# First norm block turned on VectorE, and first products of a pair accumulated in PSUM, in a linear-attention and Mish MLP block

## The chip, the cores and the metric

One NeuronCore of a Trainium2 chip runs one launch of the kernel. The metric is the device time of a run in microseconds. The kernel before took 486.94 us (median of 3 runs, 486.89 to 487.25).

## The reference

x is 2048 x 512 in float32; 32 heads of 16; the MLP has 1792 hidden units.

```python
mod = (_silu(c) @ w_mod).reshape(c.shape[0], 6, 1, -1)
sa, ca, ga, sb, cb, gb = (mod[:, 0], mod[:, 1], mod[:, 2], mod[:, 3], mod[:, 4], mod[:, 5])
h = _layernorm(x, axis=-1) * (1 + ca) + sa
x = x + ga * _A_ref(h, A_wqkv, A_wo)          # linear attention
h = _layernorm(x, axis=-1) * (1 + cb) + sb
x = x + gb * _B_ref(h, B_w1, B_b1, B_w2)      # Dense -> Mish -> Dense
```

In the attention, phi(t) is t + 1 for positive t and exp(t) otherwise, plus 1e-6; the numerator is phi(q) times the 16 x 16 sums of phi(k) v, the denominator phi(q) times the sums of phi(k).

## The kernel before

The rows are worked in four blocks b of 512 (0 to 3), each of four tiles t of 128 rows. Every matrix product is made of three products of halves: a float32 operand is split into an upper half "h" (a copy that ScalarE rounds, line 82) and a lower half "l" (the difference, on VectorE, line 88), and h·h, h·l and l·h are summed in a PSUM bank.

The order of the work is that of the program text: each engine takes its instructions in the order in which the code issues them. Side work is written as generators; `spawn` queues one and each `tick` (line 57) lets every queued generator issue its next step, so side work falls between units of TensorE. DMAs are issued by SyncE (SP), by GpSimd (POOL) and a few by ScalarE.

The stages, by the trace's clock: first layer norm, k, and the sums of phi(k) with x to 107 us; the q product of blocks 0 and 1 in seven products instead of eight (`q_sevens`, line 380) to 127; attention and output units `o_unit(b, t)` (line 920), with the q products of blocks 2 and 3 between them, to 205; the MLP of blocks 0 and 1 to 348, and of blocks 2 and 3 to the end.

An output unit multiplies the normalised q of a block, in halves qs (line 902), with a combined matrix m: twelve products of 128 x 512. The normalised q needs the reciprocal of the denominator, which goes out to DRAM as `rden_d` and comes back spread over partitions in four loads `rd` (`attend`, line 877; for blocks 2 and 3 SyncE issues them).

The second layer norm of block 0 is made by `norm_first` (line 927): ScalarE sums, VectorE and GpSimd make the scale, ScalarE applies it to `n_0_t`. Then the columns of the four tiles have to become rows for the MLP's products. For blocks 0 and 1, `transpose_f` (line 986) does that with four 128 x 128 turns on TensorE into a bank, from which ScalarE scales to `hf` (line 991). The table `order` (line 1080) says ahead of which output unit n = 4b + t each (block, quarter of the columns) is turned. For blocks 2 and 3, VectorE turns 32 x 32 squares into a tile `wide` (`turn`, line 235), four DMAs write them to DRAM (`spread`, line 241), four loads bring them back as rows (`load_squares`, line 249), and ScalarE scales (`turned_f`, line 982, line 256). The scaled quarters are split as b11, b21, b12, b22, and `columns` (line 996) makes the differences t1 to t4.

The hidden units are worked in pairs g of two tiles, the two blocks together by a scheme of seven products. In `pair_begin` (line 1151) the product a11·b11 goes into a bank `pa`; ScalarE copies it to SBUF as `u1`, the product a12·b21 goes into another bank, and VectorE adds the two (line 1158) before Mish. Later products s2·t2, s3·t3 and a22·t4 are accumulated onto `pa`, with ScalarE copies `u2` and `u3` between. `pair_unit` (line 1197) puts two units of the second matrix (`d_unit`, line 1116, or in the second half of the MLP `e_unit`, line 1347) between these products. `q_sevens` has the same scheme with `u1` in SBUF.

PSUM's eight banks have tags: acc four, h three, tp one.

Of the kernel before, what the change touches and what calls it, by code (L numbers as in the profile page):

```python
# [10 lines left out]
AF = mybir.ActivationFunctionType  # L11
# [14 lines left out]
def block_kernel(ctx: ExitStack, tc: tile.TileContext, x, wqkv, wo, w1, b1t, w2, c, wmodt, out):  # L26
# [352 lines left out]

    def q_sevens(side):  # L380

        pa, pc, u1, u2, u3 = {}, {}, {}, {}, {}

        def result(b, g, p, u):
            if u is not None:
                c = sb(f"cq_{b}_{g}")
                dve.tensor_tensor(c, p, u, op=ALU.add)
                p = c
            pq[b, g] = sb(f"q_{b}_{g}")
            spawn(phi(p, f"q_{b}_{g}", pq[b, g], u is not None))  # L390

        def copy(p, name):
            u = sb(name)
            act.activation(u, p, AF.Copy)
# [12 lines left out]
        for o in range(2):  # L407
            q_product(o, "s3", "t3", onto=pa[o])
            u3[o] = copy(pa[o], f"qu3_{o}")
        side(3)  # L410
        for o in range(2):
            result(0, 2 + o, q_product(o, "a22", "t4", onto=pa[o]), None)
        side(4)
        for o in range(2):
            pc[o] = q_product(o, "s1", "t1", ("h", "acc")[o])
            result(1, 2 + o, pc[o], u3[o])
        side(5)
        for o in range(2):
            q_product(o, "s4", "b22", onto=pc[o])
            result(1, o, pc[o], u2[o])  # L420
        side(6)
# [504 lines left out]

    def norm_first(t):

        yield
        sums = act_sums("n", 0, t, xt["r", 0, t])  # L930
        yield
        sums_eps("n", 0, t, sums)
        yield
        sums_shift("n", 0, t, sums)
        yield
        v = xt["n", 0, t] = sb(f"n_0_{t}")
        ln_apply("n", 0, t, xt["r", 0, t], v, act)

    def norm_each(b, t):

# [136 lines left out]
                tick()  # L1077
    act.preload_act_table_set("mish")

    order = {8: [(0, 0), (0, 2)], 9: [(0, 1)], 10: [(0, 3), (1, 0)], 11: [(1, 2)], 12: [(1, 1)], 13: [(1, 3)]}  # L1080
    for b in range(1, NB):
        for t in range(4):
            n = 4 * b + t
            for i, j in order.get(n, ()):
                transpose_f(i, j, "h")
                spawn(split_b(i, j, f"b{j // 2 + 1}{i + 1}"))
            if n in (12, 13):
                spawn(columns(0, n - 12, ("b11", "b12", "b21", "b22")))
            if n == 14:
                break  # L1090
            o_unit(b, t)
            if b == 1:
                spawn(norm_each(1, t))
            if n == 4:
                load_w2(0)
                load_w2(1)
            if n == 5:
                spawn(attend(3, 3, sp))
            if n == 7:
                spawn(w2_job(0))  # L1100
                spawn(w2_job(1))
                load_w2(2)
                load_w2(3)
            tick()
# [45 lines left out]

    def pair_begin(c0, g, tags):

        u1, pa = sb(f"u1_{g}"), product(g, "a11", "b11", tags[0])
        act.activation(u1, pa, AF.Copy)  # L1154
        c11, p = sb(f"c11_{g}"), product(g, "a12", "b21", tags[1])

        def result():
            add(c11, p, u1)
            yield
            yield from mish(c11, c0, 2 * g)  # L1160

        spawn(result())
        return pa

    def result_b(p, u, f):

# [4 lines left out]

    def pair_early(g, pa, tag):
# [34 lines left out]
    def two_pairs(c0, g0, g1, begun, between):  # L1209

        s0 = pair_early(g0, begun[0], "h")
        tick()
        pc = product(g1, "s1", "t1", "h")
        pair_middle(g0, *s0)
        tick()
        pa = begun[1]
# [322 lines left out]
```

## Time and profile before

| | us |
|---|---|
| median of the runs | 486.94 |
| the profiled execution | 487.57 |
| its span, first to last instruction | 485.9 |
| TensorE (PE) busy | 478.1 |
| VectorE (DVE) busy | 403.9 |
| ScalarE (ACT) busy | 305.6 |
| GpSimd (POOL) busy | 120.2 |

A row of a timeline has the start in us, the length in us, engine, line, operation, output<-inputs, shapes and count; in brackets, how long the engine had been idle and what ended that. PE is TensorE, DVE VectorE, ACT ScalarE, SPq the queue of SyncE that issues DMAs. Consecutive matmuls overlap, so the step from one start to the next counts. A row of the table of stages has, after the stage, its length, and the busy time of PE, of its weight loads (PEld), of DVE, ACT and POOL with counts, then the granted clock, the DMA engines' share and GB/s. A row of a DMA queue has packets, MB and the share of the 16 DMA engines.

### The profile page before, as it was taken

What the parts mean: (1) busy time and instruction counts of PE and PEld (TensorE: products, weight loads), DVE (VectorE), ACT (ScalarE), POOL (GpSimd) and SP (SyncE); (2) the same over time, 40 slices, a digit from 0 to 9 for tenths busy, and PEclk for the clock granted to TensorE, in tenths of its full rate; (3) what the DMA queues carried; (4) which work ended last, traced back from release to release, by engine and by line L of the source; (5) the groups of instructions that cost most, each with busy time, mean ns of one, the idle gap of its engine ahead of it and who ended that gap; (6) DMA issues with size and microseconds to landing.
All of it is one profiled execution on the core that took longest, in us unless ns stands there. A gap on an engine that the chain in (4) does not pass through costs nothing.

```text
span 485.9 us, 7068 instructions
## 1 busy us (share of the span) xinstructions
PE 478.1 (98%) x2322; PEld 390.8 (80%) x2322; DVE 403.9 (83%) x801; ACT 305.6 (63%) x551; POOL 120.2 (25%) x200
## 2 busy tenths in 40 slices
PE   7999999999999999999999999999999999999997
PEld 6688877767887888888888888888888888888887
DVE  6999898998999899988998883699345878879992
ACT  6786468755764979557887664795064667657600
POOL 3673121000022213113434225133011101454400
PEclk9999999999999999999999999999999999999999
DMA  8904859553865328258649539998352602687974
GB/s 305 379 10 82 200 102 263 203 146 92 272 172 152 92 74 258 86 175 282 219 148 266 168 108 263 378 327 209 126 149 78 125 16 65 152 194 156 235 153 108
DMA packets 81023, 84.90 MB, mean 175 GB/s; under 512 B 22705, under 2 KB 54969, under 8 KB 80986
## 3 DMA queue, kind: packets, MB, share of 16 engines
q1 hardware_dynamic: 55944, 49.17, 35.0%
q0 software_dynamic: 22784, 34.49, 26.6%
q10 hardware_dynamic: 2258, 0.79, 0.8%
q8 instruction: 18, 0.29, 0.2%
q14 instruction: 19, 0.16, 0.1%
HBM read 57.42 MB, written 24.91 MB: 169 GB/s over the span
## 4 chain that ended last, share of the span: by engine, by line
PE 83%; DMA 6%; DVE 6%; SPq 2%; ACT 1%; POOL 1%; issue 0%; DVEq 0%; ACTq 0%
PE p_a L1144 20%; PE p_s L1144 8%; PE oacc L75 5%; PE oacc L74 5%; PE oacc L76 5%; PE m L76 5%; PE m L74 5%; PE m L75 5%; PE o L74 3%; PE o L76 3%; PE o L75 3%; DMA sq_x<-wide_x 3%; DMA wm<-in_wmodt_dram 2%; PE pq_a L376 2%; PE pq L74 2%; PE pq L76 1%
## 5 line engine op out<-in xcount | busy, mean ns | idle before, releaser
L1154 ACT ACTIVATE u<-p_a 128x512 f32<-128x512 f32 x14 | 8.4, 599 | 29.5 <-PE p_a L1144 29.5
L776 POOL DMA_DIRECT2D wb<-w2d x14 | 9.8, 704 | 67.4 <-PE p_a L1144 16.9
L1149 DVE TENSOR_TENSOR cb<-p_s,u 128x512 f32<-128x512 f32 x28 | 19.2, 688 | 7.5 <-ACT u L1185 7.5
L1136 ACT ACTIVATE ub<-cb,b1c 128x512 f32<-128x512 f32 x28 | 20.1, 720 | 6.8 <-DVE cb L1149 6.7
L199 POOL TENSOR_TENSOR rs_n<-rs_n,half 128x1 f32<-128x1 f32 x16 | 9.8, 611 | 55.7 <-DVE rs_n L225 42.8
L1179 ACT ACTIVATE u<-p_a 128x512 f32<-128x512 f32 x12 | 7.2, 599 | 25.0 <-PE p_a L1144 25.0
L1435 POOL DMA_DIRECT2D wt_m<-w2t x20 | 14.0, 702 | 25.4 <-PE m L76 17.0
L889 POOL DMA_DIRECT2D rden_d<-rden x2 | 1.5, 736 | 60.1 <-DVE rden L887 60.1
L782 POOL DMA_DIRECT2D w2b<-w2d x20 | 10.6, 538 | 20.6 <-PE oacc L76 14.5
L1111 ACT ACTIVATE u<-p_a,b1c 128x512 f32<-128x512 f32 x14 | 9.6, 688 | 8.7 <-PE p_a L1144 8.6
L1149 DVE TENSOR_TENSOR c<-p_a,u 128x512 f32<-128x512 f32 x14 | 9.5, 688 | 5.7 <-PE p_a L1144 5.0
L1185 ACT ACTIVATE u<-p_a 128x512 f32<-128x512 f32 x14 | 8.3, 591 | 6.9 <-PE p_a L1144 6.5
L290 DVE SCALAR_TENSOR_TENSOR ku<-e_k,relu_k 128x512 f32<-128x512 f32 x16 | 11.3, 708 | 1.5 <-ACT relu_k L288 1.5
L290 DVE SCALAR_TENSOR_TENSOR q<-e_q,relu_q 128x512 f32<-128x512 f32 x16 | 10.7, 690 | 1.2 <-ACT relu_q L288 1.2
L199 POOL TENSOR_TENSOR rs_x<-rs_x,half 128x1 f32<-128x1 f32 (+1 forms) x10 | 7.8, 786 | 15.1 <-DVE rs_x L194 14.3
L190 DVE BATCH_NORM_STATS2 st_x<-x 128x6 f32<-128x512 f32 x13 | 8.8, 677 | 3.1 <-DMA x<-in_x_dram 3.1
L913 DVE TENSOR_TENSOR r<-o,r 128x512 f32<-128x512 f32 x16 | 10.9, 680 | 0.5 <-PE o L76 0.5
L287 ACT ACTIVATE e_k<-pk 128x512 f32<-128x512 f32 x16 | 9.4, 586 | 2.7 <-PE pk L76 2.7
L901 DVE SCALAR_TENSOR_TENSOR q<-q,rd 128x512 f32<-128x512 f32 x16 | 10.5, 691 | 0.2 <-DMA rd<-rden_d 0.2
L1127 DVE TENSOR_TENSOR r<-oacc,r 128x256 f32<-128x256 f32 x8 | 3.4, 425 | 8.8 <-PE oacc L76 8.8
L175 DVE SCALAR_TENSOR_TENSOR wm<-wm,sc_row 128x512 f32<-128x512 f32 x16 | 10.5, 688 | 0.0
L299 POOL DMA_DIRECT2D ku<-ku x8 | 7.2, 940 | 13.5 <-DVE ku L290 13.5
(1580 smaller groups left out, 1898.7 us busy)
## 6 DMA issues: line engine op xcount, KB each, us to landing
wm<-in_wmodt_dram SPq DMA_DIRECT2D x24, 256.0 KB, 5.8
w1p<-in_w_dram SPq DMA_DIRECT2D x24, 256.0 KB, 4.3
w2b<-w2d POOLq DMA_DIRECT2D x20, 256.0 KB, 6.8
wt_m<-w2t POOLq DMA_DIRECT2D x20, 256.0 KB, 3.6
r<-in_x_dram SPq DMA_DIRECT2D x16, 256.0 KB, 2.9
x<-in_x_dram SPq DMA_DIRECT2D x15, 256.0 KB, 4.7
w2r<-in_w_dram SPq DMA_DIRECT2D x14, 256.0 KB, 7.7
wb<-w2d POOLq DMA_DIRECT2D x14, 256.0 KB, 3.5
```

The costliest lines, as they stand in the source:

```text
L74: pe.matmul(o, st[0], mv[0], start=start, stop=False)
L75: pe.matmul(o, st[0], mv[1], start=False, stop=False)
L76: pe.matmul(o, st[1], mv[0], start=False, stop=stop)
L175: dve.scalar_tensor_tensor(t, t, 1.0, row, op0=ALU.mult, op1=ALU.mult, accum_out=mc[:, i:i + 1])
L199: pool.tensor_tensor(y, y, half[:, lo:hi], op=ALU.pow)
L290: dve.scalar_tensor_tensor(dst, e, 1.0, r, op0=ALU.min, op1=ALU.add)
L782: pool.dma_start(w2s[f][i], w2d[f // 2, i][:, f % 2, :])
L913: dve.tensor_tensor(r, p, r, op=ALU.add)
L1136: act.activation(u, p, AF.Mish, bias=b1c[:, f:f + 1])
L1144: pe.matmul(p, st, mv, start=onto is None and c == 0 and i == 0, stop=c == 1 and i == 2, skip_group_check=onto is not None)
L1149: dve.tensor_tensor(out, p, u, op=ALU.add)
L1435: pool.dma_start(v, w2t[g][:, :, SUM[name], :])
```

## The change

Three things are changed.

First, block 0's second norm is turned on VectorE, spread and loaded back, as blocks 2 and 3 are; `norm_first` starts one tick earlier and issues the turns, the spread and the loads of squares; the table `order` is rewritten, and block 1 is still turned on TensorE. Second, ScalarE's copy of a11·b11 goes into the PSUM bank of the second product, a12·b21 is accumulated onto it, and the sum on VectorE goes; so in `q_sevens` and in every pair. In a pair, a12·b21 moves behind the first unit of the second matrix (in the first two pairs behind the output units that stand there), and s1·t1 behind s2·t2. Third, the split b12 of block 1's first half, which no product uses, is left out; the differences t1 to t4 of blocks 0 and 1 are issued after the output unit of their place rather than ahead of it.

```diff
     def q_sevens(side):
...
         for o in range(2):
             pa[o] = q_product(o, "a11", "b11", "h")
-            u1[o] = copy(pa[o], f"qu1_{o}")
+            p11[o] = ps(("h", "tp")[o], f"pq_11_{o}")
+            act.activation(p11[o], pa[o], AF.Copy)
         side(0)
         for o in range(2):
-            p = q_product(o, "a12", "b21", ("h", "tp")[o])
-            result(0, o, p, u1[o])
+            q_product(o, "a12", "b21", onto=p11[o])
+            result(0, o, p11[o], None)
             q_product(o, "s2", "t2", onto=pa[o])
...
     def norm_first(t):
-        yield
         sums = act_sums("n", 0, t, xt["r", 0, t])
         yield
         sums_eps("n", 0, t, sums)
         yield
         sums_shift("n", 0, t, sums)
-        yield
-        v = xt["n", 0, t] = sb(f"n_0_{t}")
+        v = sb(f"n_0_{t}")
         ln_apply("n", 0, t, xt["r", 0, t], v, act)
+        yield
+        turn("n", 0, t, v)
+        if t == 3:
+            yield
+            spread("n", 0)
+            for _ in range(3):
+                yield
+            for j in (0, 2, 1, 3):
+                load_squares("n", 0, j)
...
-    order = {8: [(0, 0), (0, 2)], 9: [(0, 1)], 10: [(0, 3), (1, 0)], 11: [(1, 2)], 12: [(1, 1)], 13: [(1, 3)]}
+    order = {9: [(0, 0), (0, 2)], 10: [(1, 0)], 11: [(0, 1), (1, 2)], 12: [(0, 3), (1, 1)], 13: [(1, 3)]}
...
             for i, j in order.get(n, ()):
-                transpose_f(i, j, "h")
-                spawn(split_b(i, j, f"b{j // 2 + 1}{i + 1}"))
-            if n in (12, 13):
-                spawn(columns(0, n - 12, ("b11", "b12", "b21", "b22")))
+                if i:
+                    transpose_f(i, j, "h")
+                else:
+                    turned_f(i, j)
+                if (i, j // 2) != (1, 0):
+                    spawn(split_b(i, j, f"b{j // 2 + 1}{i + 1}"))
             if n == 14:
                 break
             o_unit(b, t)
+            if n in (12, 13):
+                spawn(columns(0, n - 12, ("b11", "b12", "b21", "b22")))
...
     def pair_begin(c0, g, tags):
-        u1, pa = sb(f"u1_{g}"), product(g, "a11", "b11", tags[0])
-        act.activation(u1, pa, AF.Copy)
-        c11, p = sb(f"c11_{g}"), product(g, "a12", "b21", tags[1])
...
+        pa, p11 = product(g, "a11", "b11", tags[0]), ps(tags[1], f"p11_{g}")
+        act.activation(p11, pa, AF.Copy)
+        return pa, p11
...
+    def pair_first(c0, g, p11):
+        m = mish(product(g, "a12", "b21", onto=p11), c0, 2 * g)
+        next(m)
+        spawn(m)
+
+    def pair_early(c0, g, begun, tag):
+
+        pa, p11 = begun
         u2 = sb(f"u2_{g}")
-        pc = product(g, "s1", "t1", tag)
+        pair_first(c0, g, p11)
         product(g, "s2", "t2", onto=pa)
         act.activation(u2, pa, AF.Copy)
+        pc = product(g, "s1", "t1", tag)
         return pa, pc, u2
...
     def pair_unit(c0, g, odd, between):
         begun = pair_begin(c0, g, ("tp" if odd else "h", "h"))
         tick()
-        state = pair_early(g, begun, "h")
+        between[0]()
+        state = pair_early(c0, g, begun, "h")
         tick()
-        between[0]()
         pair_middle(g, *state)
```

Where instructions move, in the order of issue. A name has block or group and tile first and a running number last: `qs_3_0h` is the upper half of block 3's first q tile, `hf_n_0_2` block 0's third quarter after scaling, `sq_n` the squares, `tp_n` a bank of turns, `w2` halves of the second matrix.

ScalarE behind the halves of w2, ahead of the output units of block 3; before:

```order
L82 ACTIVATE w2_1h_2248<-w2g_1_2209 128x512
L82 ACTIVATE b11_0_0h_2251<-hf_n_0_0_2217 128x512
L82 ACTIVATE b21_0_2h_2254<-hf_n_0_2_2224 128x512
L991 ACTIVATE hf_n_0_1_2263<-tp_n_0_1_2258,mc_143 128x512
L82 ACTIVATE qs_3_0h_2279<-q_3_0_1800 128x512
L82 ACTIVATE qs_3_1h_2283<-q_3_1_1840 128x512
```

ScalarE at the same place, now:

```order
L82 ACTIVATE w2_1h_2246<-w2g_1_2213 128x512
L256 ACTIVATE hf_n_0_0_2250<-sq_n_0_0_2229,mc_143 128x512
L256 ACTIVATE hf_n_0_2_2252<-sq_n_0_2_2231,mc_143 128x512
L82 ACTIVATE qs_3_0h_2268<-q_3_0_1794 128x512
L82 ACTIVATE qs_3_1h_2272<-q_3_1_1834 128x512
L82 ACTIVATE b11_0_0h_2279<-hf_n_0_0_2250 128x512
L82 ACTIVATE b21_0_2h_2282<-hf_n_0_2_2252 128x512
```

The scalings of block 0's first and third quarter stood ahead of w2's halves; they now stand between those and block 3's first halves, and their splits behind these.

SyncE from block 3's reciprocal on; before:

```order
L889 DMA rden_d_3_2156<-rden_3_2153 4x32x128
L893 DMA rd_3_0_2158<-rden_d_3_2156 128x1x512
L893 DMA rd_3_1_2160<-rden_d_3_2156 128x1x512
L893 DMA rd_3_2_2162<-rden_d_3_2156 128x1x512
L893 DMA rd_3_3_2164<-rden_d_3_2156 128x1x512
L704 DMA w2r_2_2186<-in_w2_dram 128x512
L704 DMA w2r_3_2188<-in_w2_dram 128x512
L790 DMA w1p_2_0_2556<-in_w1_dram 128x4x128
```

SyncE at the same place, now:

```order
L245 DMA sq_n_0_2099<-wide_n_0_1976 32x16x128 x4
L890 DMA rden_d_3_2160<-rden_3_2157 4x32x128
L894 DMA rd_3_0_2162<-rden_d_3_2160 128x1x512
L894 DMA rd_3_1_2164<-rden_d_3_2160 128x1x512
L894 DMA rd_3_2_2166<-rden_d_3_2160 128x1x512
L894 DMA rd_3_3_2168<-rden_d_3_2160 128x1x512
L705 DMA w2r_2_2190<-in_w2_dram 128x512
L705 DMA w2r_3_2192<-in_w2_dram 128x512
L252 DMA sq_n_0_0_2229<-sq_n_0_2099 128x512
L252 DMA sq_n_0_2_2231<-sq_n_0_2099 128x512
L252 DMA sq_n_0_1_2233<-sq_n_0_2099 128x512
L252 DMA sq_n_0_3_2235<-sq_n_0_2099 128x512
```

The spread of block 0 now goes ahead of `rden_d`, and the loads of its squares behind the two loads of w2.

VectorE around the lower halves of block 3's first output unit; before:

```order
L88 TENSOR_TENSOR qs_3_0l_2280<-q_3_0_1800,qs_3_0h_2279 128x512
L88 TENSOR_TENSOR qs_3_1l_2284<-q_3_1_1840,qs_3_1h_2283 128x512
L901 SCALAR_TENSOR_TENSOR q_3_2_2000<-q_3_2_2000,rd_3_2_2162 128x512
L901 SCALAR_TENSOR_TENSOR q_3_3_2033<-q_3_3_2033,rd_3_3_2164 128x512
L88 TENSOR_TENSOR b11_0_1l_2293<-hf_n_0_1_2263,b11_0_1h_2292 128x512
L913 TENSOR_TENSOR r_2_2_1501<-o_2_2_2310,r_2_2_1501 128x512
L88 TENSOR_TENSOR qs_3_2l_2327<-q_3_2_2000,qs_3_2h_2326 128x512
L88 TENSOR_TENSOR qs_3_3l_2331<-q_3_3_2033,qs_3_3h_2330 128x512
```

VectorE at the same place, now:

```order
L88 TENSOR_TENSOR qs_3_0l_2269<-q_3_0_1794,qs_3_0h_2268 128x512
L88 TENSOR_TENSOR qs_3_1l_2273<-q_3_1_1834,qs_3_1h_2272 128x512
L902 SCALAR_TENSOR_TENSOR q_3_2_2007<-q_3_2_2007,rd_3_2_2166 128x512
L902 SCALAR_TENSOR_TENSOR q_3_3_2037<-q_3_3_2037,rd_3_3_2168 128x512
L88 TENSOR_TENSOR b11_0_0l_2280<-hf_n_0_0_2250,b11_0_0h_2279 128x512
L88 TENSOR_TENSOR b21_0_2l_2283<-hf_n_0_2_2252,b21_0_2h_2282 128x512
L914 TENSOR_TENSOR r_2_2_1495<-o_2_2_2293,r_2_2_1495 128x512
L88 TENSOR_TENSOR qs_3_2l_2310<-q_3_2_2007,qs_3_2h_2309 128x512
L88 TENSOR_TENSOR qs_3_3l_2314<-q_3_3_2037,qs_3_3h_2313 128x512
```

The lower halves b11_0_0 and b21_0_2, which stood ahead of qs_3_0l, now stand between it and qs_3_2l; b11_0_1l has moved behind.

More of the change, by code (lines that the diff above doesn't have):

```diff
@@ L380, in q_sevens @@
     def q_sevens(side):
-        pa, pc, u1, u2, u3 = {}, {}, {}, {}, {}
+        pa, pc, p11, u2, u3 = {}, {}, {}, {}, {}
         def result(b, g, p, u):
@@ L934, in norm_first @@
         sums_shift("n", 0, t, sums)
+        v = sb(f"n_0_{t}")
+        ln_apply("n", 0, t, xt["r", 0, t], v, act)
         yield
-        v = xt["n", 0, t] = sb(f"n_0_{t}")
-        ln_apply("n", 0, t, xt["r", 0, t], v, act)
+        turn("n", 0, t, v)
[6 more added lines that the diff above has]
+                load_squares("n", 0, j)
     def norm_each(b, t):
@@ L1151, in pair_begin @@
     def pair_begin(c0, g, tags):
-        u1, pa = sb(f"u1_{g}"), product(g, "a11", "b11", tags[0])
-        act.activation(u1, pa, AF.Copy)
-        c11, p = sb(f"c11_{g}"), product(g, "a12", "b21", tags[1])
-        def result():
-            add(c11, p, u1)
-            yield
-            yield from mish(c11, c0, 2 * g)
-        spawn(result())
-        return pa
+        pa, p11 = product(g, "a11", "b11", tags[0]), ps(tags[1], f"p11_{g}")
+        act.activation(p11, pa, AF.Copy)
+        return pa, p11
     def result_b(p, u, f):
@@ L1170, in result_b @@
         mish_b(c, f)
-    def pair_early(g, pa, tag):
+    def pair_first(c0, g, p11):
[4 more added lines that the diff above has]
+        pa, p11 = begun
         u2 = sb(f"u2_{g}")
-        pc = product(g, "s1", "t1", tag)
+        pair_first(c0, g, p11)
         product(g, "s2", "t2", onto=pa)
         act.activation(u2, pa, AF.Copy)
+        pc = product(g, "s1", "t1", tag)
         return pa, pc, u2
@@ L1209, in two_pairs @@
     def two_pairs(c0, g0, g1, begun, between):
-        s0 = pair_early(g0, begun[0], "h")
+        s0 = pair_early(c0, g0, begun[0], "h")
         tick()
@@ L1215, in two_pairs @@
         tick()
-        pa = begun[1]
+        pa, p11 = begun[1]
+        pair_first(c0, g1, p11)
         u2 = sb(f"u2_{g1}")
```

## Prediction

> **What bounds the kernel now.** I read the page's head first, then a table of stages, then TensorE, ScalarE, VectorE and SyncE in order of time around 180 to 200 us, where the change moves work. From the page, the span and TensorE's busy time and clock; from the table of stages, TensorE's column against the length of each stage:
>
> ```profile
> span 485.9 us, 7068 instructions
> PE 478.1 (98%) x2322; PEld 390.8 (80%) x2322; DVE 403.9 (83%) x801; ACT 305.6 (63%) x551; POOL 120.2 (25%) x200
> ...
> PEclk9999999999999999999999999999999999999999
> ```
>
> ```profile
> 180.00:200.10 20.10, 20.10 (x106) 16.86 (x105) 19.73 (x41) 17.09 (x28) 6.26 (x12) 1.00 0.59 184
> 200.10:300.00 99.90, 99.90 (x443) 82.73 (x442) 83.76 (x176) 67.39 (x124) 31.55 (x58) 1.00 0.64 193
> 348.00:435.00 87.00, 87.00 (x384) 71.71 (x383) 61.78 (x113) 51.69 (x88) 16.09 (x23) 1.00 0.49 121
> ```
>
> TensorE is busy for the whole of each stage, at full clock. So the end moves only by what is taken out of TensorE's stream or by a gap put into it; work taken off another engine is worth nothing unless a gap goes with it, and there is none to go.
>
> **What leaves TensorE: 16 turns.** TensorE in order of time; the twelve o products between two groups of turns are cut to their first rows:
>
> ```profile
> 177.29 0.39 PE L74 MATMUL o<-m_0h,qs_0h 128*128 128x512 f32 x1
> ...
> 180.02 1.03 PE L989 MATMUL tp_n<-ident,n 128*128 128x128 f32 x8
> 180.81 0.48 PE L74 MATMUL o<-m_0h,qs_0h 128*128 128x512 f32 x1
> ...
> 183.63 0.60 PE L989 MATMUL tp_n<-ident,n 128*128 128x128 f32 x4
> ...
> 186.82 1.03 PE L989 MATMUL tp_n<-ident,n 128*128 128x128 f32 x8
> ...
> 193.97 0.48 PE L74 MATMUL o<-m_0h,qs_0h 128*128 128x512 f32 x1
> ...
> 196.83 0.60 PE L989 MATMUL tp_n<-ident,n 128*128 128x128 f32 x4
> ...
> 200.01 0.39 PE L1144 MATMUL p_a<-b_0h,a_0h 128*128 128x512 f32 x1
> ```
>
> Twelve products alone take 180.02 - 177.29 = 2.73 us. With eight turns they take 183.63 - 180.02 = 3.61, so eight turns cost 0.88; with four, 186.82 - 183.63 = 3.19, so four cost 0.46. The sixteen that go (the first eight, the next four, half of the eight at 186.82) cost 0.88 + 0.46 + 0.44 = **1.8 us**. All stand ahead of the unit o(3,0) (block 3, tile 0), which starts at 193.97 and has issued its last product when the turns at 196.83 begin. It would start at 192.2 and end at 195.0 if its operands are there.
>
> **What comes in their place, and when it is there.** Its operands are the halves qs_3. ScalarE, VectorE and SyncE around them, each in order of time:
>
> ```profile
> 186.20 0.62 ACT L82 ACTIVATE w_1h<-w2g 128x512 fp32r<-128x512 f32 x1
> ...
> 188.42 0.62 ACT L82 ACTIVATE qs_0h<-q 128x512 fp32r<-128x512 f32 x1
> 188.94 0.62 ACT L82 ACTIVATE qs_1h<-q 128x512 fp32r<-128x512 f32 x1
> ```
>
> ```profile
> 169.60 0.69 DVE L290 SCALAR_TENSOR_TENSOR q<-e_q,relu_q 128x512 f32<-128x512 f32 x1 [0.75 <-ACT relu_q L288]
> 170.82 0.69 DVE L913 TENSOR_TENSOR r<-o,r 128x512 f32<-128x512 f32 x1 [0.52 <-PE o L76]
> ...
> 185.72 0.69 DVE L901 SCALAR_TENSOR_TENSOR q<-q,rd 128x512 f32<-128x512 f32 x1 [0.23 <-DMA rd<-rden_d]
> ...
> 189.34 0.68 DVE L88 TENSOR_TENSOR qs_0l<-q,qs_0h 128x512 fp32r<-128x512 f32 x1
> 189.94 0.69 DVE L88 TENSOR_TENSOR qs_1l<-q,qs_1h 128x512 fp32r<-128x512 f32 x1
> 190.54 1.29 DVE L901 SCALAR_TENSOR_TENSOR q<-q,rd 128x512 f32<-128x512 f32 x2
> ...
> 193.54 0.69 DVE L88 TENSOR_TENSOR qs_3l<-q,qs_3h 128x512 fp32r<-128x512 f32 x1
> ```
>
> ```profile
> 178.00 0.58 SPq L889 DMA_DIRECT2D rden_d<-rden  x1
> 180.53 2.55 SPq L893 DMA_DIRECT2D rd<-rden_d  x4
> 183.18 0.89 SPq L704 DMA_DIRECT2D w2r<-in_w_dram  x2
> 209.05 0.93 SPq L790 DMA_DIRECT2D w1p<-in_w_dram  x2
> ```
>
> Now the two scalings hf_n_0_0 and hf_n_0_2 of loaded squares stand on ScalarE right ahead of qs_3_0h. An engine takes its instructions in turn, so qs_3_0h waits for those squares, though it doesn't use them. The squares are issued by SyncE behind rden_d of block 3, its four rd loads and two w2r loads. Step by step:
>
> 1. Four turns of block 0 come onto VectorE ahead of the reciprocal for block 3, at 0.60 each by the step between its rows: 2.4 us. Part goes into idle time like the 0.75 and 0.52 above, but the last turn needs n_0_3, which ScalarE makes only behind e_q, relu, a_1h and s_1h. I take the reciprocal, and so rden_d, 1.3 us late: 179.3 instead of 178.00. The bounds are 0 and 2.4, and the spread of 1 MB, now ahead of rden_d in SyncE's queue, speaks for the upper one.
> 2. SyncE's queue then carries, in order, what it carried before. Two views of the transfers, one for 181 to 190.1 us and one for 190.1 to 200, give the queue's packets and MB:
>
> ```profile
> q1 hardware_dynamic: 830, 1.57, 61.9%
> ```
>
> ```profile
> q1 hardware_dynamic: 2, 0.00, 0.0%
> ```
>
> 1.57 MB are the six loads of 0.26 MB (rd and w2r); they are through by 190, in 8.5 us, or 1.4 us each. Late by 1.3, they are through at 191.3; the first square has landed at 192.7, the second at 194.1. From a load's last byte to the engine's start I take 0.5 us: the second rd load, through at 184.3 by this rate from 181.5 on, let VectorE start its q at 185.72, so the bounds are 0 and 1.4. ScalarE's second scaling starts at 194.6 and takes 0.80, to **195.4**.
> 3. From there the two engines have to catch up on what they did earlier before: ScalarE qs_3_0h (0.6), then VectorE nine instructions at 0.60 until qs_3_3l (qs 0 and 1, q 2 and 3, b11, b21, an o sum, qs 2 and 3), because two of the new lower halves stand ahead of qs_3_2l: 6.0 us. With the last product of 0.23 (2.73 / 12), o(3,0) ends 6.25 after 195.4, at **201.65** instead of 196.83. Behind it, turns and o(3,1) follow as before and the first block product starts 4.8 us late. Its operand b11_0_1l comes two VectorE instructions behind qs_3_3l, 1.2 us, in time for it. The tightest later one, t2's second half, comes 21 instructions behind, 12.6 us, and TensorE gets to it 13.8 us after the end of o(3,0), by its order: 1.2 spare.
>
> That is 4.8 us net, the 1.8 us saved included: a hole of 6.6 us in TensorE's stream. Nothing gives it back, since TensorE is full from there on.
>
> How sure is the landing? Squares of the first norm, loaded while other queues wrote, held ScalarE in this trace; SyncE's row is the issue, ScalarE's the first use. Beside them, the shortest landing of the later squares, from their tile's view:
>
> ```profile
> 52.35 3.28 SPq L252 DMA_DIRECT2D sq_x<-sq_x  x4
> ```
>
> ```profile
> 56.95 0.82 ACT L256 ACTIVATE hf_x<-sq_x,mc 128x512 f32<-128x512 f32 x1 [5.80 <-DMA sq_x<-sq_x]
> ```
>
> ```profile
> DMA to landing us min/median/max: 3.0/6.7/10.3
> ```
>
> 4.6 us from issue to use, and a wait of 5.80 us: the same kind of wait as I forecast. The least is 3.0 us.
>
> The granted clock above is 1.0 throughout. The longest gap of TensorE in this trace, first of its waits, is short:
>
> ```profile
> PE warm L136 <- POOL ones L130: 1.1, 1, 1.1
> ```
>
> The Trainium skill, page TensorE: Matmul & The Clock Gate, section Part 1: The HAM clock gate, says that about 3.4 us without work put the array at half clock, until it has been busy that long again. The trace can't confirm this, having no such gap; my gap of 192.2 to 196 would be about that long. By the rule the sum would be some 1.7 us more, by the row of the clock nothing.
>
> **The pairs.** The copy of p_a moves from SBUF into a bank. This is ScalarE's row for these copies on the page, and then, inside one pair, a norm tile's sums (first and last row), mish, a_h and u3 copy:
>
> ```profile
> L1154 ACT ACTIVATE u<-p_a 128x512 f32<-128x512 f32 x14 | 8.4, 599 | 29.5 <-PE p_a L1144 29.5
> ```
>
> ```profile
> 230.45 0.64 ACT L220 ACTIVATE scrap_n<-r 128x512 f32<-128x512 f32 x1 [0.47 <-DMA w2t<-t_0l]
> ...
> 231.84 0.18 ACT L221 ACTIVATION_READ_ACCUMULATOR scrap_n<-r,sums_n 128x1 f32 x1
> ...
> 236.47 0.71 ACT L1111 ACTIVATE u<-c,b1c 128x512 f32<-128x512 f32 x1
> 237.22 0.63 ACT L82 ACTIVATE a_4h<-u 128x512 fp32r<-128x512 f32 x1
> 237.76 0.58 ACT L1185 ACTIVATE u<-p_a 128x512 f32<-128x512 f32 x1
> ```
>
> ScalarE stands idle 2.1 us (29.5 / 14) ahead of each such copy, so it starts as soon as the product ends. Into a bank no row shows a copy; I take 0.60 as into SBUF, between 0.58 (shortest row of that size here) and 0.82 (longest). Cover is one product of 1.36 us in block 2's pairs and in the q stage, 2.7 us or more elsewhere; even 0.82 fits, and without cover each would cost its 0.60. VectorE loses 14 + 2 sums and, with the unused split, two lower halves, ScalarE two upper halves: no gap goes with them, so 0. The wait that is new: s3 accumulates onto p_a after the u2 copy, which now stands behind mish and a_h. From the end of a12, ScalarE needs 0.75 + 0.54 + 0.60 = 1.9 us, and TensorE has s2 and s1, 2.7 us, until s3: 0.8 spare, cost 0. In four pairs a norm tile's sums stand ahead of mish (232.02 - 230.45 = 1.6 us); should they make ScalarE late by their whole length, s3 waits 0.8 us each time.
>
> **Rivals.**
> - *Early squares, faster.* The queue doesn't hold the squares back. With the second issued at 186.3 (184.07 + 1.3 + two issues) and the least landing of 3.0, ScalarE is through at 190.1 and o(3,0) ends at 196.4: 0.5 us gained; without the 1.3, all 1.8. It turns at a second square landed by 189.8. Against it: the queue's 1.57 MB until 190. 485.1 to 486.4.
> - *Landing as at 52.35.* 4.6 us after an issue at 185.4, and 1.4 more for the second: ScalarE through at 192.2, +1.6 us, 488.5.
> - *The clock falls after the hole.* The turns and o(3,1), 200.01 - 196.83 = 3.2 us, run at half speed: +3.2 on the forecast, 494.9. For it only the gap's length, against it the clock's row. It is the rule of the Trainium skill's page TensorE: Matmul & The Clock Gate, weighed above.
> - *Pairs wait.* 0.8 us in four pairs, +3.2 on the forecast, 494.9; in all ten, 499.7. Against it the 0.8 spare and ScalarE's 69 us of work in 100 in the table (67.39 in 99.90).
>
> **How the numbers follow.** The profiled run took 487.57 us, of which 485.9 are span; it lies 0.6 above the median of 486.94 of the runs, and the difference is applied to the median: 486.94 + 4.8 = **491.7 us**. Chances: forecast 0.57 (its own range 489.5 to 493.8, by 0 and 2.4 us of lateness and a queue 1 us faster or slower), clock 0.12, landing as at 52.35 0.11, early squares 0.15, pairs 0.05. The range leaves out the early squares and the pairs: 487.4 to 495.0. 0.2% (1.0 us) is about what a measurement of this kernel can tell from no change. Faster by over that, two thirds of the early squares: 0.10; within it, the rest of them: 0.05; slower: 0.85.
>
> **What the profile after would show.** No transposes ahead of o(2,0); ScalarE idle for 5 us or more before hf_n from sq_n at L256, released by a DMA; TensorE idle, in all 6 to 7 us, before products of o(3,0), released by qs_3; the queue's loads through near 191; the pairs without a gap and DVE down by 18 instructions less four turns. I am wrong if the squares land before 190 us, if a gap shows in the pairs, or if products behind the hole run at lower clock.

## The result, and the profile after

The changed kernel takes 494.52 us (median of 4 runs, 492.53 to 495.6) against 487.01 (486.89 to 487.25): a ratio of 1.0149, interval 1.0114 to 1.0184, 7.5 us more. The profiled execution took 495.13 us, 7.56 more than that of before (487.57).

The page's head and clock row, and the table of stages:

```profile
span 493.4 us, 7017 instructions
PE 478.7 (97%) x2306; PEld 389.5 (79%) x2306; DVE 394.9 (80%) x787; ACT 305.9 (62%) x549; POOL 120.3 (24%) x200
...
PEclk9999999999999999899999999999999999999999
```

```profile
180.00:205.00 25.00, 18.47 (x80) 13.51 (x78) 15.44 (x35) 12.70 (x22) 5.95 (x10) 0.93 0.57 182
205.00:300.00 95.00, 95.00 (x422) 78.66 (x420) 81.12 (x172) 67.09 (x123) 26.67 (x49) 1.00 0.60 184
```

TensorE's busy time is nearly what it was (478.7 us; 478.1 before). The loss lies in one stage: 18.47 us of work in 25.00, at a mean clock of 0.93. From 205 to 300 us TensorE is again full at full clock. Its longest waits name the place:

```profile
PE o L74 <- ACT qs_0h L82: 4.8, 1, 4.8
...
PE o L76 <- DVE qs_2l L88: 1.1, 1, 1.1
```

ScalarE and SyncE there, and then TensorE, in order of time:

```profile
195.90 0.81 ACT L256 ACTIVATE hf_n<-sq_n,mc 128x512 f32<-128x512 f32 x1 [7.81 <-DMA sq_n<-sq_n]
197.27 0.81 ACT L256 ACTIVATE hf_n<-sq_n,mc 128x512 f32<-128x512 f32 x1 [0.56 <-DMA sq_n<-sq_n]
197.99 0.61 ACT L82 ACTIVATE qs_0h<-q 128x512 fp32r<-128x512 f32 x1
```

```profile
179.28 0.59 SPq L890 DMA_DIRECT2D rden_d<-rden  x1
181.80 2.60 SPq L894 DMA_DIRECT2D rd<-rden_d  x4
184.50 0.88 SPq L705 DMA_DIRECT2D w2r<-in_w_dram  x2
185.47 2.87 SPq L252 DMA_DIRECT2D sq_n<-sq_n  x4
```

```profile
185.75 0.27 PE L997 MATMUL tp_n<-ident,n 128*128 128x128 f32 x1
186.39 0.44 PE L997 MATMUL tp_n<-ident,n 128*128 128x128 f32 x2 [0.37 <-ACT n L208]
187.10 0.33 PE L997 MATMUL tp_n<-ident,n 128*128 128x128 f32 x1 [0.27 <-ACT n L208]
...
193.25 0.60 PE L997 MATMUL tp_n<-ident,n 128*128 128x128 f32 x4
198.65 0.68 PE L74 MATMUL o<-m_0h,qs_0h 128*128 128x512 f32 x1 [4.80 <-ACT qs_0h L82]
199.13 0.63 PE L75 MATMUL o<-m_0l,qs_0h 128*128 128x512 f32 x1
199.56 0.63 PE L76 MATMUL o<-m_0h,qs_0l 128*128 128x512 f32 x1
...
203.59 0.50 PE L76 MATMUL o<-m_2h,qs_2l 128*128 128x512 f32 x1 [1.09 <-DVE qs_2l L88]
...
204.62 0.60 PE L997 MATMUL tp_n<-ident,n 128*128 128x128 f32 x4
...
207.83 0.39 PE L1156 MATMUL p_a<-b_0h,a_0h 128*128 128x512 f32 x1
```

Read them as one chain. SyncE issues the squares from 185.47 on, behind rd and w2r. ScalarE stands idle 7.81 us, released by a DMA, scales twice and is through at 197.27 + 0.81 = 198.08; only then does it make qs_3_0h, which never needed a square. TensorE, ready after the turns at 193.25, starts o(3,0) at 198.65. The first block product starts at 207.83 instead of 200.01: 7.8 us late, nearly as much as the end (493.4 - 485.9 = 7.5).

The chain has a simple form, which the experiments use. Take the end of the second scaling, row's start plus length, from the execution's time: 495.13 - 198.08 = 297.05 us. The forecast had 487.57 + 4.8 - 195.4 = 296.97. So what follows the scaling was forecast to 0.1 us in sum, with some luck: it took 0.3 us more up to the first block product and 0.3 less behind that (495.13 - 207.83 = 287.30, before 487.57 - 200.01 = 287.56). The scaling itself came 2.7 us later than forecast.

### The profile page after: what moved, and what is told of

Its sections match the earlier page's. It is cut to its first block, busy times and chain, and to the rows that moved or that the text cites. A ratio compares the mean times of both kernels' runs of the same rounds, so it can differ in the third digit from the quotient of the medians.

```text
span 493.4 us, 7017 instructions
## 1 busy us (share of the span) xinstructions
PE 478.7 (97%) x2306; PEld 389.5 (79%) x2306; DVE 394.9 (80%) x787; ACT 305.9 (62%) x549; POOL 120.3 (24%) x200
## 4 chain that ended last, share of the span: by engine, by line
PE 67%; DVE 16%; DMA 9%; ACT 3%; SPq 2%; issue 2%; POOL 1%; DVEq 0%; ACTq 0%
PE p_a L1156 15%; PE p_s L1156 8%; PE oacc L76 5%; PE oacc L75 5%; PE oacc L74 5%; PE m L76 5%; PE m L74 5%; PE m L75 5%; PE p L1156 4%; DMA sq_x<-wide_x 3%; DMA wm<-in_wmodt_dram 2%; PE pq_a L376 2%; DMA sq_n<-sq_n 2%; DVE wm L175 2%; DVE q L902 2%
## 5 line engine op out<-in xcount | busy, mean ns | idle before, releaser
L1166 ACT ACTIVATE p<-p_a 128x512 f32<-128x512 f32 x14 | 8.1, 582 | 25.3 <-PE p_a L1156 13.3
L1123 ACT ACTIVATE u<-p,b1c 128x512 f32<-128x512 f32 x14 | 9.6, 688 | 16.8 <-PE p L1156 16.8
L1196 ACT ACTIVATE u<-p_a 128x512 f32<-128x512 f32 x14 | 8.4, 598 | 16.9 <-PE p_a L1156 16.8
L256 ACT ACTIVATE hf_n<-sq_n,mc 128x512 f32<-128x512 f32 x12 | 9.3, 804 | 8.4 <-DMA sq_n<-sq_n 8.4
L290 DVE SCALAR_TENSOR_TENSOR ku<-e_k,relu_k 128x512 f32<-128x512 f32 x16 | 11.3, 704 | 1.6 <-ACT relu_k L288 1.6
L74 PE MATMUL o<-m_0h,qs_0h 128*128 128x512 f32 x16 | 7.0, 437 | 4.8 <-ACT qs_0h L82 4.8
L902 DVE SCALAR_TENSOR_TENSOR q<-q,rd 128x512 f32<-128x512 f32 x16 | 10.4, 682 | 1.2 <-DMA rd<-rden_d 1.2
L919 POOL DMA_DIRECT2D x1d<-r x8 | 4.4, 548 | 27.0 <-DVE r L914 27.0
```

The lines of the kernel that those rows point to most:

```text
L74: pe.matmul(o, st[0], mv[0], start=start, stop=False)
L290: dve.scalar_tensor_tensor(dst, e, 1.0, r, op0=ALU.min, op1=ALU.add)
L902: dve.scalar_tensor_tensor(t, t, TINY, rd[g], op0=ALU.add, op1=ALU.mult)
L1123: act.activation(u, p, AF.Mish, bias=b1c[:, f:f + 1])
```

## Experiments

Three theories stood after the result. The first: ScalarE's order makes qs_3 wait for squares that come late, and nothing else is lost. The second: the pairs carry part of the loss. The third: the lower clock behind the hole carries it (its rival in the prediction had 494.9, nearly what was measured). Each kernel's ratio is to the kernel before, run beside it.

### Each half of the change alone

One kernel has only the edits of `q_sevens` and of the pairs:

```diff
-            u1[o] = copy(pa[o], f"qu1_{o}")
+            p11[o] = ps(("h", "tp")[o], f"pq_11_{o}")
+            act.activation(p11[o], pa[o], AF.Copy)
...
-        act.activation(u1, pa, AF.Copy)
+        act.activation(p11, pa, AF.Copy)
```

> The kernel before with only the pairs and the q stage changed (copy of a11·b11 into the second bank, a12·b21 accumulated onto it, the new order inside a pair); block 0's turns as before. Theory: none of the 7.5 us is here, because ScalarE and VectorE have slack beside each product: 487.0 us, within 486.5 to 487.5, and no row of TensorE's waits from s3 or a12 in a pair. Rival: the pairs carry the part of the loss that the forecast did not have (7.5 - 4.8 = 2.7 us): 489 us or more, with TensorE's waits on the u2 copy at line 1165 or so.

The other has only those of `norm_first`, of the table `order`, of the split and of the place of the differences:

```diff
-    order = {8: [(0, 0), (0, 2)], 9: [(0, 1)], 10: [(0, 3), (1, 0)], 11: [(1, 2)], 12: [(1, 1)], 13: [(1, 3)]}
+    order = {9: [(0, 0), (0, 2)], 10: [(1, 0)], 11: [(0, 1), (1, 2)], 12: [(0, 3), (1, 1)], 13: [(1, 3)]}
...
+        turn("n", 0, t, v)
```

> The kernel before with only block 0's turns on VectorE, the new order table, the differences after the output unit, and without the unused split; pairs and q stage as before. Theory: the whole loss is ScalarE waiting for the squares ahead of qs_3_0h: 494.5 us (492.5 to 495.6), TensorE idle some 5 us before o(3,0) by qs_0h. Rival that the pairs cost 2.7 us: 491.8 us.

The pairs alone: 487.18 us, ratio 0.9999 (0.9991 to 1.0008). The turns alone: 494.67 us, 1.0154 (1.0141 to 1.0167). TensorE's longest waits, first of the pairs, then of the turns:

```profile
PE warm L136 <- POOL ones L130: 1.1, 1, 1.1
```

```profile
PE o L74 <- ACT qs_0h L82: 4.5, 1, 4.5
```

In the first the longest wait is the one at the start of the program, which was there before; no pair has one as long as that, and the time is that of before. The whole loss is in the turns, and the second theory falls.

### TensorE kept at work in the hole

```diff
+            if n == 12:
+                fill = ps("tp", "fill")
+                for i in range(20):
+                    pe.matmul(fill, ms[0][0][:, 0:P], ms[1][0], start=i == 0, stop=i == 19)
             o_unit(b, t)
```

> The changed kernel with 20 products of 128x512 more, ahead of o(3,0), into the bank that is free there and read by nobody: 20 x 0.23 = 4.6 us, inside the hole of 4.8 us. They keep TensorE at work while it waits, so that o(3,0) should run at full clock. Theory (the slow clock costs little, because o(3,0)'s last six products wait for the lower halves from VectorE at 202.85 and 203.45 anyway): o(3,0)'s first products step by 0.23 instead of 0.43 us, its end moves from 204.6 to about 204.2: 494.1 us. Rival (the clock after the hole is 2.7 us of the loss): 491.8 us. If the step stays at 0.43 us, the slow step is no matter of idle time.

494.55 us, 1.0156 (1.0142 to 1.0169): the same as without. TensorE around o(3,0):

```profile
193.29 4.80 PE L1104 MATMUL fill<-m_1h,m_0h 128*128 128x512 f32 x20
197.98 0.50 PE L74 MATMUL o<-m_0h,qs_0h 128*128 128x512 f32 x1
...
199.05 0.40 PE L74 MATMUL o<-m_1h,qs_1h 128*128 128x512 f32 x1
199.28 0.39 PE L75 MATMUL o<-m_1l,qs_1h 128*128 128x512 f32 x1
199.51 0.40 PE L76 MATMUL o<-m_1h,qs_1l 128*128 128x512 f32 x1
200.72 0.50 PE L74 MATMUL o<-m_2h,qs_2h 128*128 128x512 f32 x1 [0.81 <-ACT qs_2h L82]
...
202.91 0.50 PE L76 MATMUL o<-m_2h,qs_2l 128*128 128x512 f32 x1 [1.46 <-DVE qs_2l L88]
...
203.96 0.60 PE L997 MATMUL tp_n<-ident,n 128*128 128x128 f32 x4
```

The products now step by 0.23 us (199.05, 199.28, 199.51), in the changed kernel by 0.43 (199.13, 199.56). So the slow step comes with the idle time. But the time is no shorter, because the faster products wait for qs_2h and qs_2l instead. ScalarE's second scaling ended at 197.41 here and the turns behind o(3,0) start at 203.96, 6.55 us later; in the changed kernel it is 204.62 - 198.08 = 6.54. The third theory falls for this execution: VectorE's catch-up sets the end of o(3,0) here, at either clock. Where the slow stretch lasts longer it does cost time, as the part on the prediction shows.

### The squares' place in SyncE's queue

The first attempt issued the two w2r loads one tick later. The squares are issued at the next tick, so SyncE's order stayed what it was, and the run repeats the changed kernel:

```diff
-                load_w2(2)
-                load_w2(3)
             tick()
+            if n == 7:
+                load_w2(2)
+                load_w2(3)
```

> The changed kernel with the two loads of w2 (tiles 2 and 3) issued behind the loads of block 0's squares instead of ahead of them; nothing else moves. Theory (the squares' place in SyncE's queue sets the end of ScalarE's wait): 0.52 MB less ahead of them, two loads at 1.4 us, so ScalarE is through its second scaling near 195.2 instead of 198.0, and near 192 if the squares are then also out before GpSimd's stores start at 191; o(3,0) ends 2.8 to 6 us earlier: 488.5 to 491.7 us. Rival (each load has a round trip of its own and the queue's order does not matter): 494.5 us, ScalarE's wait ending within 1 us of 197. Rival (the wait is for the spread in DRAM, not for the loads): 494.5 us as well, with the landing unchanged.

493.03 us (491.23 to 495.62), 1.0121 (1.0097 to 1.0146). That the same order of instructions varies by 4 us, where the kernel before beside it varies by 1.3 (486.56 to 487.88), is of use below. The second attempt has `n == 8` in that place and puts the squares ahead:

> The changed kernel with the two w2 loads issued one tick later still, now truly behind the four loads of block 0's squares in SyncE's queue; nothing else moves. Theory (place in the queue): SyncE issues the squares 0.9 us earlier, and 0.52 MB less is ahead of them: in the changed kernel the second scaling ended 12.3 us (11.5 to 12.5 in four profiles) after the first square's issue; without two loads at 1.4 us it should end 9.5 us after it or sooner, some 3.7 us earlier: 489.5 to 491.5 us. Rival (the trip of the squares is as long whatever stands ahead): only the 0.9 us of the issue, 493.6 us.

492.33 us, 1.0106 (1.0092 to 1.0121): earlier, but by less than the theory's 3 to 5 us. SyncE and ScalarE:

```profile
183.82 1.77 SPq L252 DMA_DIRECT2D sq_n<-sq_n  x4
185.69 2.43 SPq L705 DMA_DIRECT2D w2r<-in_w_dram  x2
```

```profile
193.00 0.81 ACT L256 ACTIVATE hf_n<-sq_n,mc 128x512 f32<-128x512 f32 x1 [5.67 <-DMA sq_n<-sq_n]
194.26 0.81 ACT L256 ACTIVATE hf_n<-sq_n,mc 128x512 f32<-128x512 f32 x1 [0.45 <-DMA sq_n<-sq_n]
```

From the squares' issue to the end of the second scaling it is still 195.07 - 183.82 = 11.25 us, against 12.6, though half a megabyte less stood ahead of them. The place in the queue was not the main thing. (The medians fell by 2.2 us, of which the earlier issue, 5.3 us behind rden_d's instead of 6.2, accounts for 0.9.)

### Stores on GpSimd's queue

What else moved at that time shows in the transfers of the changed kernel. First 183 to 191 us, then 191 to 196:

```profile
q1 hardware_dynamic: 899, 1.71, 75.2%
```

```profile
q0 software_dynamic: 500, 1.04, 61.0%
q1 hardware_dynamic: 470, 0.85, 50.0%
```

SyncE's queue (q1) had moved 1.71 MB by 191, the six loads of 1.57 MB as forecast and half of the first square. Then GpSimd's queue (q0) comes in, with its stores of x1 and of w2's halves, and takes the larger share of the engines.

By its bytes, though, q1 was not late. The six loads and two squares are 2.10 MB; from 191 to 193.5 us it moved

```profile
q1 hardware_dynamic: 289, 0.52, 60.3%
```

which makes 2.23 MB. If the queue moves its loads in the order of issue, the second square's last byte passed near 193 us, ahead of the 194.1 of the forecast, and the second scaling started over 4 us behind it (197.27). What was long is the time from the last byte to the use. No view shows the landing of a single load, so why it was long is not shown by these rows.

The next two kernels take stores out of this stretch, and a third puts more in. The four stores of w2 five ticks later:

```diff
+        if f < 2:
+            for _ in range(5):
+                yield
         for i in range(2):
             pool.dma_start(w2d[g, i][:, n, :], w2s[f][i])
```

> The changed kernel with GpSimd's four stores of w2's halves (1.05 MB) put five ticks later, so that they no longer share the DMA engines with the squares between 191 and 198 us; GpSimd's stores of x1 stay. Theory (contention with GpSimd's stores made the squares 2.5 us later than the queue's own rate would have): the second scaling ends 1.5 to 2.5 us earlier: 492 to 493 us. Rival (the queue's own order sets it): 494.5 us, and the time from the squares' issue to the second scaling's end stays at 12.3 us.

493.61 us, 1.0128 (1.0109 to 1.0147). Then also the stores of block 2's rows of x1, five ticks later:

```diff
         if b >= 2:
-            yield
+            for _ in range(6 if b == 2 else 1):
+                yield
```

> The changed kernel with all of GpSimd's stores of that stretch later: the four of w2's halves by five ticks, and those of block 2's x1 rows by five ticks. GpSimd's queue then carries next to nothing while the squares come. Theory (the squares are late because they share the DMA engines with GpSimd's stores): the second scaling ends 9 us or less after the squares' issue, against 12.5 in the changed kernel and 9.5 with the four stores out, and the time is that of the forecast or a little under: 490.5 to 492 us. Rival (the stores shifted the landing in one profile only, by chance): 493.5 us or more, as in the other runs of that order.

492.32 us, 1.0106 (1.0085 to 1.0126). And the four stores made twice:

```diff
         for i in range(2):
+            if f < 2:
+                pool.dma_start(drp.tile([P, 2, D], F32R, name=f"w2e_{f}_{i}")[:, n, :], w2s[f][i])
             pool.dma_start(w2d[g, i][:, n, :], w2s[f][i])
```

> The changed kernel with the four stores of w2's halves made twice, the second time to a place in DRAM that nobody reads: 1.05 MB more on GpSimd's queue from 188 us on. Theory (sharing): 1.05 MB fewer gave 2.8 us earlier squares, so as much more should make them later by 1.5 to 3 us: 496 to 497.5 us. Rival (GpSimd's stores do not matter): 494.5 us and the second scaling's end 12.5 us behind the squares' issue.

493.48 us, 1.0116 (1.01 to 1.0131). ScalarE's scalings in the three, in that order:

```profile
193.20 1.52 ACT L256 ACTIVATE hf_n<-sq_n,mc 128x512 f32<-128x512 f32 x2 [5.30 <-DMA sq_n<-sq_n]
```

```profile
191.65 1.52 ACT L256 ACTIVATE hf_n<-sq_n,mc 128x512 f32<-128x512 f32 x2 [4.54 <-DMA sq_n<-sq_n]
```

```profile
195.26 0.81 ACT L256 ACTIVATE hf_n<-sq_n,mc 128x512 f32<-128x512 f32 x1 [7.63 <-DMA sq_n<-sq_n]
196.65 0.81 ACT L256 ACTIVATE hf_n<-sq_n,mc 128x512 f32<-128x512 f32 x1 [0.57 <-DMA sq_n<-sq_n]
```

| kernel | squares issued | second scaling over | between | time of the profiled execution | less the scaling's end |
|---|---|---|---|---|---|
| changed | 185.47 | 198.08 | 12.6 | 495.13 | 297.05 |
| the same order again | 183.96 | 195.53 | 11.6 | 492.52 | 296.99 |
| turns alone | 184.60 | 196.92 | 12.3 | 494.21 | 297.29 |
| fillers | 185.16 | 197.41 | 12.3 | 494.45 | 297.04 |
| squares ahead | 183.82 | 195.07 | 11.3 | 492.12 | 297.05 |
| four stores later | 185.26 | 194.72 | 9.5 | 492.36 | 297.64 |
| all stores later | 184.47 | 193.17 | 8.7 | 490.84 | 297.67 |
| four stores twice | 185.01 | 197.46 | 12.5 | 496.14 | 298.68 |

With stores out, the squares are there 2 to 4 us sooner after their issue in these profiles, one for each kernel. Worked out from each trace as above, the time from the second square's last byte to the second scaling's start is 3.7 to 4.5 us in the six kernels with all stores in place and 1.6 or 1.7 us in the two with stores later. But the first kernel of the next section has its stores in place too, and there the second scaling is over 193.81 + 0.81 - 184.40 = 10.2 us after the issue, and that time is 2.7 us. So the stores are the likeliest cause, and chance has a part that single profiles can't measure.

With more stores the squares are no later: the last expectation missed. From 191 to 196 us q0 then moved 1.19 MB instead of 1.04, though 1.05 MB were added; the rest came behind the squares. The Trainium skill, page DMA: Bandwidth & Descriptors, section Queues, rings and completion order, says that each engine serves the queues that have work for it in turn, packet by packet. The trace agrees as far as it goes: both queues move in the same stretch, and a longer line of stores takes no larger share. With the four stores made twice q0 had 70.6% of the engines from 191 to 196 us, and 61.0 to 77.0% in the four kernels with them made once and SyncE's order unchanged (changed, fillers, turns alone, the same order again).

In the time the effect is not shown. The medians fall from 494.5 to 493.6 and 492.3, each above what was expected of it. But the same order again has 493.0 and the four stores twice 493.5, all these intervals overlap with that of the changed kernel, and the runs of one kernel differ by up to 4 us. What the stores cost in a mean run stays open.

### The scalings out of qs_3's way

```diff
-    order = {9: [(0, 0), (0, 2)], 10: [(1, 0)], 11: [(0, 1), (1, 2)], 12: [(0, 3), (1, 1)], 13: [(1, 3)]}
+    order = {10: [(1, 0)], 11: [(0, 0), (0, 2), (0, 1), (1, 2)], 12: [(0, 3), (1, 1)], 13: [(1, 3)]}
```

> The changed kernel with the two scalings of block 0's first and third quarter placed two output units later (ahead of o(2,3) instead of o(2,1)), so that on ScalarE all four upper halves qs_3 stand ahead of them; the loads stay as they are. Theory (qs_3_0h had no need of the squares, only its place in ScalarE's order made it wait): the wait of 4.8 us by qs_0h goes, o(3,0) starts behind the turns near 193. The squares still land near 197.3, and the first block product, at about 199 now, needs their halves b11: 1 to 3 us of wait there instead: 487 to 490 us. Rival (qs_3 is late for another reason, its rd loads or VectorE): the wait by qs_0h stays, 493 us or more.

490.89 us (487.86 to 492.54), 1.0071 (1.0047 to 1.0095). The wait by qs_0h is gone, so it was ScalarE's order that tied qs_3 to the squares. But some 3.5 us of the loss remain, more than expected (487 to 490 us): the squares are also late for the products that do need them. What is late next shows in TensorE's first wait; the profiled execution is the fastest of the six:

```profile
PE p_a L1156 <- DVE t_1l L88: 1.5, 1, 1.5
```

This product is s2·t2 of the first pair, and what it lacks is the lower half of t2's second half: the operand that the prediction had as the tightest, with 1.2 us to spare. VectorE makes it in turn, behind the lower halves of b11 and b21 and the differences, all of which wait for the squares. With the squares also ahead of the w2 loads:

> The changed kernel with both: the squares' loads ahead of the two w2 loads, and the two scalings two output units later. Theory: no wait is left between 185 and 205 but the 0.6 to 1.0 us by which block 1's turns now come before their tiles; of the 1.8 us of turns some 0.8 to 1.2 remain as gain: 485.8 to 486.5 us (before 486.95). If the first block product still waits for b11: up to 488. Rival (the turns through DRAM cost TensorE something else): above 488.

486.33 us (485.71 to 488.83), 0.9995 (0.9981 to 1.0009). TensorE's one longer wait from 185 us on and its first block product, 1.1 us ahead of before:

```profile
PE tp_n L997 <- ACT n L208: 0.7, 2, 0.4
```

```profile
198.91 0.39 PE L1157 MATMUL p_a<-b_0h,a_0h 128*128 128x512 f32 x1
```

Eight runs took 485.7 to 486.7 us and four 488.1 to 488.8; together that is no difference from before. Two more kernels looked for the longer runs' cause, first with the four stores of w2 later as well:

> The kernel of both moves (squares ahead of w2, scalings ahead of o(2,3)), and GpSimd's four stores of w2's halves five ticks later. In both moves 8 of 12 runs took 485.7 to 486.7 us and 4 took 488.1 to 488.8. Theory (in the longer runs the squares land later because they share the DMA engines with the stores, and the first block product waits): with the stores gone from that stretch no run is over 487.5, median 485.7 to 486.4, at or below before by 0.6 to 1.3. Rival (the longer runs come from elsewhere): runs over 488 remain, median as in both moves, 486.3.

487.56 us (486.22 to 489.16), 1.0015 (1.0002 to 1.0027): half of the runs are over 488, so the stores are not what makes them long. Then with block 1's first turns one unit later:

```diff
-    order = {10: [(1, 0)], 11: [(0, 0), (0, 2), (0, 1), (1, 2)],
+    order = {11: [(1, 0), (0, 0), (0, 2), (0, 1), (1, 2)],
```

> The kernel of three moves, with block 1's first turns ahead of o(2,3) instead of o(2,2), so that its tiles n_1 are there. Theory (the 0.7 us by which TensorE waits for n_1 in both moves was part of the 1.8 us of turns that the change freed): the wait goes, 0.5 to 0.7 us less than three moves: 485.0 to 485.9 us. Rival (the scaling hf_n_1_0 then comes later on ScalarE, and the first differences or the first block product wait instead): same as three moves or more, with a wait of p_a or of the turns' bank in the trace.

487.24 us (486.48 to 489.37), 1.001 (0.9999 to 1.0022), where 485.0 to 485.9 was expected. Here the profiled execution is one of the longer ones (488.02). TensorE's first wait, and then ScalarE and VectorE ahead of it:

```profile
PE p_a L1160 <- DVE t_1l L88: 1.5, 1, 1.5
```

```profile
192.64 0.76 ACT L1002 ACTIVATE hf_n<-tp_n,mc 128x512 f32<-128x512 f32 x1
193.30 2.21 ACT L256 ACTIVATE hf_n<-sq_n,mc 128x512 f32<-128x512 f32 x3
```

```profile
191.31 0.69 DVE L905 SCALAR_TENSOR_TENSOR q<-q,rd 128x512 f32<-128x512 f32 x1 [0.39 <-DMA rd<-rden_d]
```

The wait for n_1 is gone, as expected, and t2's second half is late by 1.5 us. The squares are not what it lacks: ScalarE makes three scalings of them in a row and waits for none. They start 14.8 us behind the issue of rden_d, in the kernel of three moves 13.2. Of these 1.6 us, 0.9 come from block 3's q tiles, for which VectorE waited on two late rd loads (0.64 us at 186.63 and 0.39 at 191.31; with three moves 0.16 us and none), and 0.7 from block 1's scaling, which now stands ahead at 192.64. The second is what the recorded rival named. Whether the longer runs of the other kernels lose their 2 us in the same way was not settled: their profiles are of the shorter runs. No version beats the kernel before by more than the measurement tells.

## Why the prediction was right, and where not

The mechanism, its place and its sign were right: ScalarE's order made qs_3 wait for squares that came late. 491.7 us was forecast and 494.5 measured, inside the range of 487.4 to 495.0, but above the forecast's own 489.5 to 493.8; the loss was 7.5 us where 4.8 was the sum. Of its steps:

- *Turns.* TensorE was through with its turns ahead of o(3,0) at 193.25 + 0.46 = 193.7, not at 192.2. Most of the 1.8 us went where the prediction did not look: with block 0's turns gone, block 1's first turns stood waiting for n_1 (0.37 + 0.27 us), and came in pieces. From their start at 185.75 to the next o product, at 187.18, it is 1.43 us; the next four turns took 0.36 (190.04 to 190.40). So 1.1 us were lost there. In the changed kernel the hole covers this. In the version with both moves it is what remains of the difference: of the 1.1 us by which the first block product came earlier, 0.46 were there at 141 us already, ahead of all turns, so 0.6 was gained and 1.1 lost. With block 1's turns one unit later the first block product started at 197.72, with the same 0.46: there the full 1.8 us were gained.
- *Step 1.* rden_d was issued at 179.28, forecast 179.3, with a little luck: 0.3 of the 1.28 us were there at 141 us, ahead of the turns.
- *Step 2 failed in its size*: "the first square has landed at 192.7, the second at 194.1". It gave the squares the queue's own rate, 1.4 us each, and put 0.5 us from the last byte to ScalarE's start, at most 1.4: 194.6 for the second scaling. That scaling started at 197.27, 2.7 us later. The rate was right, the bytes being there near 193 by the working above; the 0.5 us was over 4 us. With the four stores of w2 moved, the second scaling started at 193.96 (its end, 194.72, less 0.76 by the pair's 1.52), 8.7 us after the issue, where the forecast had 194.6 - 185.4 = 9.2. So what the step left out is, most likely, GpSimd's stores. Their row stood beside that of SyncE's queue in the view of 190.1 to 200 us before, and the chance that a later transfer meets them was not priced:

```profile
q0 software_dynamic: 721, 1.68, 48.7%
```

- *Step 3.* From the scaling's end to the turns behind o(3,0) 6.54 us, forecast 6.25; from there to the first block product 3.21, forecast 3.2. The sum closes: 2.7 + 0.3 = 3.0 us, and 4.8 + 3.0 = 7.8, the lateness of the first block product.
- *Pairs, cost 0.* Right: 0.9999 alone. The fourteen copies into a bank took 582 ns each by the page of the changed kernel, where 0.60 us was taken.
- *The clock.* The rival named 494.9 and the clock did fall, but it cost no time in the profiled execution, as the fillers show. That its number lay near the result is chance: its 3.2 us were to be in o(3,1), which ran at full speed (204.98 to 207.83 in the changed kernel). It decides where the slow stretch lasts longer: in the kernel with the stores twice the step stays at 0.43 until 206.1, the turns come 204.84 - 197.46 = 7.4 us behind the scaling instead of 6.5, and o(3,1) takes 3.98 us instead of 3.21. That is 1.6 us, and the 298.68 in the table. Over the runs the two go together: of the changed kernel, of the same order again and of the kernel with four stores later, the longest run (495.6, 495.6 and 495.2 us) is the one with the lowest mean clock, 0.988. Later squares make the gap longer and with it the slow stretch, so the times alone don't part the two. TensorE's turns, its last slow product and the first block product there:

```profile
204.84 1.06 PE L999 MATMUL tp_n<-ident,n 128*128 128x128 f32 x4
...
206.12 0.56 PE L75 MATMUL o<-m_0l,qs_0h 128*128 128x512 f32 x1
...
208.82 0.39 PE L1158 MATMUL p_a<-b_0h,a_0h 128*128 128x512 f32 x1
```

- *Early squares, landing as at 52.35.* Neither came: the squares took 10.4 us from issue to use, twice the 4.6 at 52.35.

## What to carry to other kernels

An instruction that waits for a load holds everything behind it on its engine, so place it by when the load lands, and behind whatever doesn't need it. Price a landing by all the queues that are busy then, not by its own queue alone, and price the time from the last byte to the use apart from the queue's rate: in most profiles with another engine's stores beside them the squares came 2 to 4 us later, though their own queue's bytes were on time. And before counting TensorE time saved as gained, look for what TensorE then reaches too early; here block 1's tiles took 1.1 of 1.8 us, and where these were mended, the second half of t2 came 1.5 us late.

## What the runs showed of the hardware

The array's clock fell after idle time only when this was long. After gaps of 0.9, 1.65 and 2.57 us (all stores later, four stores later, squares ahead) the products step by 0.23 us from the fourth on; after 3.76, 4.51, 4.66 and 4.80 us (the same order again, turns alone, four stores twice, changed) some step by 0.43. The two gaps next to the limit, of squares ahead and of the same order again:

```profile
195.64 0.50 PE L74 MATMUL o<-m_0h,qs_0h 128*128 128x512 f32 x1 [2.57 <-ACT qs_0h L82]
```

```profile
196.10 0.80 PE L74 MATMUL o<-m_0h,qs_0h 128*128 128x512 f32 x1 [3.76 <-ACT qs_0h L82]
```

The stretch after the 4.80 us of the changed kernel in the table of windows, with the granted clock, 0.66, as third last number:

```profile
198.00:203.00 5.00, 3.85 (x8) 2.06 (x8) 4.37 (x8) 5.00 (x10) 0.00 (x0) 0.66 0.03 10
```

The Trainium skill, page TensorE: Matmul & The Clock Gate, section Part 1: The HAM clock gate, puts the limit at about 3.4 us and says that the window which is watched runs freely, so that the slow stretch differs from run to run. The trace agrees with both: the limit lies between 2.57 and 3.76 us in these profiles, and after nearly equal gaps (4.80 and 4.66) the slow steps lasted until 202 us in one and 206.1 in the other.
